# Strided attention rows loaded in pieces of 64 and 8, 48 and 6, and three times 18 rows

## The chip, the cores and the metric

The kernel runs on one core of a Trainium2 chip. The metric is the device time of one execution in microseconds (us), lower is better. Times come from repeated timed runs; one further execution was recorded by the hardware profiler, and all views of the profile below are of that execution.

## The reference

Inputs are `q`, `k`, `v` of shape (8 batches, 8 heads, 576 positions, 64), and two weight matrices. Attention is sparse: heads 0 to 3 look back over at most 32 positions (local), heads 4 to 7 at every position of the same remainder modulo 32 (strided). A feed-forward layer with a squared ReLU follows.

```
mask_local   = (rel >= 0) & (rel < 32)                    # rel = query position - key position
mask_strided = (rel >= 0) & (key % 32 == query % 32)
attn = softmax(where(mask, q @ k.T / 8, -1e9)) ; a = attn @ v
x = a.transpose(0, 2, 1, 3).reshape(4608, 512)
h = x @ w_in                                              # 512 -> 2048
out = (relu(h) ** 2) @ w_out                              # 2048 -> 512, float32
```

## The kernel before

**Two kinds of work on TensorE.** The feed-forward layer is cut in nine chunks of 512 rows of `x`. For each chunk `mm1` makes 16 groups of four matmuls (128x512) with `w_in` (L707), ScalarE applies the ReLU (L713), VectorE squares it into `g_sb` (L714), and `mm2` makes 16 groups of four matmuls with `w_out` (L729). A chunk is thus 32 groups, and all of them form one list of 288 groups, numbered from 0. Between the groups a hand-written list, `PLAN`, places the steps of attention: a line such as `44: S9! D8.0 k20v` means that these steps are issued just ahead of group 44. Batch 0, whose attention must be ready before the first chunk can start, is written out in `BATCH0`. TensorE works strictly in that order, and so does every other engine on its own part of it.

**Loads.** All loads that change float32 to bfloat16 on the way are issued by GpSimd (POOL in the profile), in the order in which the steps come. Each load is given one of eight completion semaphores in turn, so a load is issued only when the load eight places ahead of it has landed; POOL stands still until then, and whatever stands behind on POOL waits with it. DMA transposes and the stores of the output are issued by SyncE (SP), also in order.

**The strided heads.** A row of 32 consecutive positions of one head is 32 x 64 = 2048 numbers. A batch has 18 such rows in each head, so 72 rows in the four strided heads. The steps that the change touches:

- `r1q`, `r1k` (`load_str_rows`, L312) and `C2q` to `C7k` (`load_str_tall`, L349) load the 72 rows of `q` or `k` into `q_t` or `k_t` (72 partitions x 2048). For batch 1 they are transposed on TensorE (`step_TS`, L321); from batch 2 on SP transposes the tile by DMA (`transpose_str`, L354, steps `X`) into `qT_s` and `kT_s`. From `kT_s` VectorE spreads the keys into `kb` (`step_K`, L365 and L368), which the scores read (`step_SS`, L574). `q_t` and `k_t` have one buffer each: the next load waits until the transpose of the last has ended.
- `U1` to `U7` (`load_v_str`) load `v` for the strided heads into `v_st` (54 partitions): the 54 rows of heads 4 to 6 (L390), and head 7 as three overlapping stretches of its 18 rows, 768 numbers each, in one transfer with a source of 3 x 18 rows (L393). VectorE spreads the tile into `vb` (`spread_v_str`, L397).
- `load_v0` loads `v` of batch 0's strided heads into `vs0`, a part of `g_sb` (L608: 72 partitions x 4 x 512), ahead of the loads of `w_in` (L425).

Other loads that the prediction names: `w_out` in four parts (L429; part i is first needed by the groups of chunk 0's `mm2` with that part), local `v` into `vl` (L418, 24 x 64 numbers on 128 partitions), local `q` and `k` into `q_l` and `k_l` (L278), which SP transposes into `qT` and `kTl` (L378).

Of the kernel before, what the change touches and what calls it, by code (L numbers as in the profile page):

```python
# [156 lines left out]
def kernel(  # L157
# [9 lines left out]
    nc = tc.nc  # L167
    B, H, S, D = q.shape
    d_model, d_ff = moe_w_in.shape
    T = B * S  # L170
    STRIDE = 32
    NA = S // STRIDE
# [3 lines left out]
    NJ = 8  # L176
    RH = STRIDE // NJ
    SP_ = RH * NA
# [4 lines left out]
    NG = 5  # L183
    NB = NP2 + NG + 1
    W3 = 3 * NA
    RW = STRIDE * D
# [65 lines left out]
    vs0 = b0[0:SP_, 0:n_s].rearrange("p (u n d) -> p u n d", u=2, d=D)  # L252
# [47 lines left out]
    NP3 = 4 * SP_ // QL  # L300
    str_rows = {}

    def load_str_rows(b, name):
        src = q if name == "q" else k
        if b == 0:
            c = 4 if name == "q" else 8
            t = w_out_b[0:QL, c:c + NP3, :]
            nc.gpsimd.dma_start(out=t, in_=src[b, 4:8].rearrange("h (p j) d -> (h p) (j d)", j=NJ)
                                .rearrange("(s p) c -> p s c", p=QL))
        else:  # L310
            t = str_rows_t[name][0:SP_]
            nc.gpsimd.dma_start(out=t, in_=src[b, 4:8].rearrange("h (m r) d -> (h m) (r d)", r=STRIDE))  # L312
        str_rows[b, name] = t

    def step_TS(b, name, g, copy):
# [30 lines left out]
    def load_str_tall(b, name):  # L346
        src = q if name == "q" else k
        t = str_rows_t[name]
        nc.gpsimd.dma_start(out=t[0:SP_], in_=src[b, 4:8].rearrange("h (m r) d -> (h m) (r d)", r=STRIDE))  # L349
        big[b, name] = t  # L350

    def transpose_str(b, name):
# [34 lines left out]

    def load_v_str(b):
        t = v_st.tile([W3, 2 * NB * D], BF16, name="v_st")
        nc.gpsimd.dma_start(out=t[:, 0:RW], in_=v[b, 4:7].rearrange("h (m r) d -> (h m) (r d)", r=STRIDE))  # L390
        src = v[b, 7]
        src = bass.AP(src.tensor, src.offset, [[2 * NG * D, 3], [RW, NA], [1, 2 * (NG + 1) * D]])
        nc.gpsimd.dma_start(out=t[:, RW:2 * NB * D], in_=src)  # L393
        v_str[b] = t

    def spread_v_str(b, par, copy):
# [3 lines left out]
    def load_v_local_sw(b):  # L400
        i = (2 * b) % NV
        t = vl_all[:, i:i + 2]
        nc.gpsimd.dma_start(out=t[32:128, :, :, :, 0:D].rearrange("p u h t d -> p (u h t) d"),
                            in_=v[b, 0:4].rearrange("h (t p) d -> p (h t) d", p=QL))
        for u in range(2):
            st.setdefault(4 * b + u, {})["v"] = t[:, u]
# [198 lines left out]

    def load_v0():
        load_v_local_sw(0)
        nc.gpsimd.dma_start(  # L608
            out=vs0.rearrange("p u n d -> p (u n d)").rearrange("p (h c) -> p h c", h=4),
            in_=v[0, 4:8].rearrange("h (p j) d -> p h (j d)", j=NJ))  # L610

    def step_N(u):
        e, hw = st[u]["e"], S // 2
# [158 lines left out]
    def run_step(word):  # L772
# [36 lines left out]
        elif op == "P":  # L809
            first_part(*([int(x) for x in y] for y in arg.split(".")))  # L810
        elif op == "H":
            shift_v_local(int(arg[:-1]), ENG[arg[-1]])
        elif op == "C":
            load_str_tall(int(arg[:-1]), arg[-1])
        elif op == "Q":
            load_qk_rows(int(arg[:-1]), arg[-1])
        elif op == "X":
            transpose_str(int(arg[:-1]), arg[-1])
        elif op == "Y":
            transpose_local(int(arg))  # L820
        elif op == "V":
            load_v_local_all(int(arg))
        elif op == "U":
            load_v_str(int(arg))
        elif op == "B":
            spread_v_str(int(arg[0]), int(arg[1]), ENG[arg[2]])
        elif op == "l":
            load_qk_local_sw(int(arg[0]), [int(x) for x in arg[2:].split("+")], arg[1])
        elif op == "r":
            load_str_rows(int(arg[0]), arg[1])  # L830
        elif op == "i":
            load_w_in(int(arg))
        elif op == "o":
            load_w_out(int(arg))
        elif op == "z":
            late_constants()
        else:
            raise ValueError(word)
# [25 lines left out]
    nc.scalar.preload_act_table_set("natural_log_exp_and_others")  # L864
    load_qk_hw(0)
    load_str_rows(0, "q")
    make_identity(nc, ident)
    load_str_rows(0, "k")
    nc.vector.memset(idle, 0.0)
    nc.vector.memset(mask_loc, 1.0)  # L870
# [21 lines left out]
    for i in range(2):  # L892
# [8 lines left out]
                            NEG, -NEG, op0=ALU.mult, op1=ALU.add)  # L901
    load_qk_local_sw(0, (1,))
    load_v0()
    for i in range(4):
        load_w_in(i)
# [34 lines left out]
    for line in PLAN.strip().splitlines():  # L940
        n, words = line.split(":")
# [40 lines left out]
```

## Time and profile before

| what | us |
|---|---|
| median of 3 timed runs | 300.25 (299.5 to 300.93) |
| the profiled execution, its own time | 298.88 |
| its span, first to last instruction | 297.2 |
| TensorE busy with matmuls (PE) | 289.2 (97%) |
| VectorE (DVE) busy | 177.9 (60%) |
| ScalarE (ACT) busy | 172.3 (58%) |
| GpSimd (POOL) busy, issuing loads included | 72.4 (24%) |

The granted clock of TensorE was 1.000 throughout. The median of the timed runs is 1.37 us above the profiled execution, and the profiled execution's own time is 1.68 us above its span. PE is TensorE's matmuls and PEld its weight loads; a name such as `PE psb L729` is the engine, the tile that is written and the line. "Idle before" is the time in which an engine stood still ahead of an instruction, and the name behind the arrow is what ended that.

### The profile page before, as it was taken

The numbers are of one execution on the slowest core, as the hardware profiler recorded it, in microseconds if no ns is written. First come the engines' busy times: TensorE is split into PE (matmuls) and PEld (weight loads), VectorE is DVE, ScalarE is ACT, GpSimd is POOL, SyncE is SP. The second block draws the span as 40 slices with busy tenths as digits, with TensorE's granted clock in tenths as the row PEclk, the third lists the DMA queues.
The fourth block names the chain that finished last, engine by engine and source line by source line (L and its number), as shares of the span: only waits on it lengthen the run. The fifth ranks groups of instructions, "written<-read, shape, count | busy, mean of one in ns | idle before, by whom it ended". The sixth has DMA issues, their size and how long they took to land.

```text
span 297.2 us, 5652 instructions
## 1 busy us (share of the span) xinstructions
PE 289.2 (97%) x2136; PEld 146.0 (49%) x2172; DVE 177.9 (60%) x460; ACT 172.3 (58%) x325; POOL 72.4 (24%) x105
## 2 busy tenths in 40 slices
PE   7999999999999999999999999999999999999996
PEld 2644555555544444544455445544554444444444
DVE  6866779677779694697267936785475534104400
ACT  3858846686667735783477447745665257217511
POOL 8846643006404027083303710000000000000000
PEclk9999999999999999999999999999999999999999
DMA  8999999999999999999999999521011100010012
GB/s 157 181 209 204 194 198 187 158 225 140 129 166 176 157 211 164 159 136 157 186 145 150 174 186 142 89 57 71 35 23 55 73 35 0 35 74 35 0 71 73
DMA packets 93131, 37.28 MB, mean 125 GB/s; under 512 B 78956, under 2 KB 87238, under 8 KB 93104
## 3 DMA queue, kind: packets, MB, share of 16 engines
q0 software_dynamic: 54448, 18.82, 58.1%
q1 hardware_dynamic: 38512, 18.03, 32.6%
q8 instruction: 17, 0.28, 0.4%
q14 instruction: 10, 0.08, 0.1%
q10 hardware_dynamic: 144, 0.07, 0.1%
HBM read 38.21 MB, written 9.44 MB: 160 GB/s over the span
## 4 chain that ended last, share of the span: by engine, by line
PE 92%; DVE 3%; ACT 2%; issue 2%; DVEq 0%; ACTq 0%
PE psb L729 39%; PE psb L707 39%; PE psb L667 2%; PE psb L453 1%; PE psb L764 1%; PE psb L588 1%; PE psb L505 1%; PE psb L754 1%; PE psb L585 1%; PE psb L574 1%; ACT r L713 1%; PE psb L550 1%; DVE g_sb L714 1%; PE psb L475 1%; PE psb L331 0%
## 5 line engine op out<-in xcount | busy, mean ns | idle before, releaser
L707 PE MATMUL psb<-xt,w_in_b 128*128 128x512 bf16 x558 | 132.1, 379 | 1.4 <-ACT xt L692 0.4
L729 PE MATMUL psb<-w_out_b,g_sb 128*128 128x512 bf16 x542 | 125.3, 379 | 1.3 <-issue 0.6
L713 ACT ACTIVATE r<-psb 128x512 bf16<-128x512 f32 x144 | 85.5, 600 | 37.5 <-PE psb L707 34.0
L714 DVE TENSOR_TENSOR g_sb<-r 128x512 bf16<-128x512 bf16 x144 | 60.7, 423 | 72.8 <-ACT r L713 71.7
L707 PEld LDWEIGHTS <-w_in_b 128*128 128x128 bf16 x576 | 53.4, 98 | 59.0 <-issue 1.6
L729 PEld LDWEIGHTS <-g_sb 128*128 128x128 bf16 x560 | 51.8, 98 | 57.2 <-DVE g_sb L714 0.3
L733 ACT COPY y<-psb 128x512 f32<-128x512 f32 x35 | 20.6, 589 | 53.2 <-PE psb L729 50.2
L598 DVE TENSOR_TENSOR xt<-psb,rv 64x144 bf16<-64x144 f32 x84 | 34.1, 406 | 8.0 <-ACT rv L591 6.8
L590 ACT ACTIVATE rv<-psb 128x432 f32<-128x432 f32 (+1 forms) x21 | 10.5, 501 | 9.8 <-PE psb L585 9.8
L673 DVE TENSOR_TENSOR x_l<-psb,rinv 96x384 bf16<-96x384 f32 x28 | 15.5, 554 | 1.0
L349 POOL DMA_DIRECT2D q_t<-in_q_dram x6 | 3.4, 567 | 43.4 <-DMA qT_s<-q_t 26.0
L604 DVE TENSOR_TENSOR xt<-psb,rv 64x270 bf16<-64x270 f32 (+1 forms) x28 | 10.9, 432 | 3.8 <-ACT rv L591 3.6
L575 ACT ACTIVATE e<-psb 128x432 bf16<-128x432 f32 (+1 forms) x21 | 10.4, 496 | 3.7 <-PE psb L574 3.7
L418 POOL DMA_DIRECT2D vl<-in_v_dram x7 | 10.3, 1475 | 8.6 <-DMA vl<-in_v_dram 6.2
L278 POOL DMA_DIRECT2D k_l<-in_k_dram x16 | 11.7, 736 | 2.8 <-PE psb L453 2.4
L278 POOL DMA_DIRECT2D q_l<-in_q_dram x16 | 11.6, 732 | 1.0 <-DMA k_l<-in_k_dram 1.0
L561 ACT ACTIVATE e<-psb 128x384 bf16<-128x384 f32 x24 | 9.6, 511 | 3.4 <-PE psb L550 3.4
L591 ACT ACTIVATE rv<-rv 128x432 f32<-128x432 f32 (+1 forms) x21 | 11.2, 533 | 0.7
L557 DVE TENSOR_TENSOR e<-e,mask_all 128x576 bf16<-128x576 bf16 x16 | 6.7, 459 | 7.2 <-ACT e L561 7.1
L667 PEld LDWEIGHTS <-e 128*128 128x128 bf16 x168 | 8.6, 101 | 4.6
L349 POOL DMA_DIRECT2D k_t<-in_k_dram x6 | 3.2, 535 | 28.0 <-DMA kT_s<-k_t 25.7
L667 PE MATMUL psb<-vl,e 128*128 128x65 bf16 x168 | 9.5, 195 | 0.1
(117 smaller groups left out, 215.9 us busy)
## 6 DMA issues: line engine op xcount, KB each, us to landing
out_dram<-y SPq DMA_DIRECT2D x35, 256.0 KB, 2.8
vl<-in_v_dram POOLq DMA_DIRECT2D x7, 384.0 KB, 12.4
w_out_b<-in_moe_w_out_dram POOLq DMA_DIRECT2D x4, 512.0 KB, 15.1
q_t<-in_q_dram POOLq DMA_DIRECT2D x7, 288.0 KB, 5.8
k_t<-in_k_dram POOLq DMA_DIRECT2D x7, 288.0 KB, 6.1
v_st<-in_v_dram POOLq DMA_DIRECT2D x7, 216.0 KB, 7.9
w_in_b<-in_moe_w_in_dram POOLq DMA_DIRECT2D x2, 704.0 KB, 13.1
k_l<-in_k_dram POOLq DMA_DIRECT2D x16, 72.0 KB, 8.1
```

The costliest lines, as they stand in the source:

```text
L278: nc.gpsimd.dma_start(out=t[:, :, hh, :], in_=src[b, 2 * p + hh].rearrange("(t p) d -> p t d", p=QL))
L590: nc.scalar.activation(rv, pn, AF.Ln)
L591: nc.scalar.activation(rv, rv, AF.Exp, scale=-1.0)
L598: nc.vector.tensor_tensor(to[:, :, NJ * part:NJ * (part + 1), par], of, by, op=ALU.mult)
L604: nc.vector.tensor_tensor(t, of[:, g:, :, lo:lo + k], by[:, g:, :, lo:lo + k], op=ALU.mult)
L667: nc.tensor.matmul(po[0:m, n, :], e[:, c:c + m], rhs[:, NL * part + n, 0:D + 1], start=True, stop=True)
L673: nc.vector.tensor_tensor(x, po[0:QL, :, 0:D], rinv[0:QL].to_broadcast([QL, NL, D]), op=ALU.mult)
L707: nc.tensor.matmul(ph, w_in_b[:, kk, 128 * ff:128 * (ff + 1)], xt[kk][:, 512 * c:512 * (c + 1)], start=(kk == order[0]), stop=(kk == order ...
L713: nc.scalar.activation(r, ph, AF.Relu)
L714: later(1, lambda: nc.vector.tensor_tensor(g[:, ff, :], r, r, op=ALU.mult))
L729: nc.tensor.matmul(py, g[:, ff, 128 * j:128 * (j + 1)], w_out_b[:, ff, :], start=(ff == 0), stop=(ff == 15))
L733: nc.scalar.copy(y, py)
```

## The change

Every load of strided rows is split in pieces. A new helper, `load_even`, splits a transfer after the largest multiple of 16 partitions: 72 rows become 64 and 8, 54 rows become 48 and 6. The load of head 7's values becomes three transfers of 18 rows. The bytes that are moved, the tiles and the order of the steps stay as they are.

```diff
+    def load_even(out, src):
+
+        n = out.shape[0] // 16 * 16
+        for r in (slice(0, n), slice(n, out.shape[0])):
+            nc.gpsimd.dma_start(out=out[r], in_=src[r])
+
     def load_str_rows(b, name):
...
             t = str_rows_t[name][0:SP_]
-            nc.gpsimd.dma_start(out=t, in_=src[b, 4:8].rearrange("h (m r) d -> (h m) (r d)", r=STRIDE))
+            load_even(t, src[b, 4:8].rearrange("h (m r) d -> (h m) (r d)", r=STRIDE))
...
     def load_str_tall(b, name):
         src = q if name == "q" else k
         t = str_rows_t[name]
-        nc.gpsimd.dma_start(out=t[0:SP_], in_=src[b, 4:8].rearrange("h (m r) d -> (h m) (r d)", r=STRIDE))
+        load_even(t[0:SP_], src[b, 4:8].rearrange("h (m r) d -> (h m) (r d)", r=STRIDE))
...
     def load_v_str(b):
         t = v_st.tile([W3, 2 * NB * D], BF16, name="v_st")
-        nc.gpsimd.dma_start(out=t[:, 0:RW], in_=v[b, 4:7].rearrange("h (m r) d -> (h m) (r d)", r=STRIDE))
-        src = v[b, 7]
-        src = bass.AP(src.tensor, src.offset, [[2 * NG * D, 3], [RW, NA], [1, 2 * (NG + 1) * D]])
-        nc.gpsimd.dma_start(out=t[:, RW:2 * NB * D], in_=src)
+        load_even(t[:, 0:RW], v[b, 4:7].rearrange("h (m r) d -> (h m) (r d)", r=STRIDE))
+        src = v[b, 7].rearrange("(m r) d -> m (r d)", r=STRIDE)
+        for g in range(3):
+            c = 2 * NG * D * g
+            nc.gpsimd.dma_start(out=t[NA * g:NA * (g + 1), RW:2 * NB * D], in_=src[:, c:c + 2 * (NG + 1) * D])
...
     def load_v0():
         load_v_local_sw(0)
-        nc.gpsimd.dma_start(
-            out=vs0.rearrange("p u n d -> p (u n d)").rearrange("p (h c) -> p h c", h=4),
-            in_=v[0, 4:8].rearrange("h (p j) d -> p h (j d)", j=NJ))
+        load_even(vs0.rearrange("p u n d -> p (u n d)").rearrange("p (h c) -> p h c", h=4),
+                  v[0, 4:8].rearrange("h (p j) d -> p h (j d)", j=NJ))
```

The lists of instructions of TensorE, VectorE, ScalarE and SyncE are the same before and after, apart from the semaphores that they wait for: who waited for one load now waits for its pieces. GpSimd issues 36 loads more, 123 in place of 87: seven each for `q`, `k` and the first 54 rows of `v`, fourteen for head 7's values, one for `vs0`. With eight semaphores in turn, eight loads are under way at most, as before, but a piece takes a place as a whole load does. After the change all pieces that `load_even` issues have line 307, and the three transfers of 18 rows line 400; lines further down are higher by 6 or 7.

## The prediction

> **What bounds the kernel now.** The page first: who is busy, and when.
>
> ```profile
> span 297.2 us, 5652 instructions
> ...
> PE   7999999999999999999999999999999999999996
> ...
> POOL 8846643006404027083303710000000000000000
> ...
> DMA  8999999999999999999999999521011100010012
> ```
>
> TensorE is full in every slice but the first and the last. The DMA engines are full too, but only up to 180 us, and POOL issues its last load at 171 us. So the question is whether PE ever waits for a load. The waits of PE, then the only wait of its weight loads that a DMA ended:
>
> ```profile
> PE psb L764 <- DVE xt L869: 1.3, 1, 1.3
> PE psb L729 <- issue: 0.6, 4, 0.2
> PE psb L505 <- DVE kTl L460: 0.4, 1, 0.4
> PE psb L648 <- ACT e L509: 0.4, 1, 0.4
> PE psb L707 <- ACT xt L692: 0.4, 1, 0.4
> ```
>
> ```profile
> PEld L331 <- DMA w_out_b<-in_k_dram: 0.3, 1, 0.3
> ```
>
> These end before 17 us, except the 0.6 of issue. PE waits for a load once, 0.3 us at 8.7 us, for rows of batch 0 that the change doesn't touch and that are issued ahead of all that it does. The other early waits are chains of ScalarE and VectorE (a copy into `xt`, an exponential). The starts of consecutive 128x512 matmuls lie 216 ns apart from 20 us to 290 us, with loads running or not, so PE gains nothing from calmer DMA engines either. Faster loads have next to nothing to win in this execution; the change matters only if a load that comes just in time now comes late.
>
> How the loads land: each counts its semaphore up sixteen times, once for each DMA engine, and the trace has the time of every count. For the 72 rows of `q_t` issued at 67.59 us the counts come at 69.45, 70.70, then fourteen from 71.36 to 73.10: one engine has no rows, one has few, fourteen have most. For `vs0` (issued 6.87) four come from 11.54 to 12.12 and twelve from 12.79 to 13.91. By the Trainium skill, "DMA: Bandwidth & Descriptors", section "Why a DMA increments its semaphore by 16 and not by 1", a load uses the largest number of engines up to 16 that divides its rows, and some direct copies from GpSimd all 16 with the rows rounded up (five each of 72); the counts agree with twelve engines for `vs0` and with the rounding for `q_t`. The unevenness adds up while the queue is full: the first and the last count of a load lie 2.3 us apart at `w_in` (landed 15.47) and 10.8 at the `k_t` that lands at 51.63.
>
> **The change part by part.** POOL first: 36 loads more to issue. The nearest rows:
>
> ```profile
> L393 POOL DMA_DIRECT2D v_st<-in_v_dram x7 | 4.4, 633 | 1.4 <-DMA xt<-in_k_dram 0.7 <-DMA xt<-in_q_dram 0.6
> L390 POOL DMA_DIRECT2D v_st<-in_v_dram x7 | 3.7, 533 | 4.8 <-DVE vb L397 1.5 <-DVE rinv L672 1.5 <-DMA w_in_b<-in_moe_w_in_dram 1.2
> L349 POOL DMA_DIRECT2D q_t<-in_q_dram x6 | 3.4, 567 | 43.4 <-DMA qT_s<-q_t 26.0 <-DMA qT<-q_l 15.9 <-DMA vl<-in_v_dram 1.4
> ```
>
> 54 rows cost 533 ns and 72 rows 567, so the rows hardly count, and a piece of 6, 8 or 18 rows is taken at 0.5 us (bounds 0.2, if the rows counted in full the way these two differ and something fixed were shared, and 0.63, the dearest row). 36 x 0.5 = 18 us on POOL: 72.4 becomes about 90 of 297. That lies beside PE; its cost is loads issued later.
>
> Start, to 17 us. `vs0` in two pieces puts the four loads of `w_in` 0.5 us later, the first from 7.61 to 8.1. It lands at 15.47, 7.9 us after its issue, because the engines work at what was issued before; it is queue-bound, and the 0.5 is hidden by that backlog. With sixteen engines even on 64 of the 72 rows I take its landing at 15.2 to 15.6. Its first matmul starts at 16.26, released by the `xt` copy of ScalarE, so both bounds cost nothing: 0.0.
>
> 17 to 52 us. Up to `w_out` part 2 six pieces more are in line (`vs0`, `q_t`, `k_t`, one of `v_st`'s 54 rows, two of head 7's), and the waits for eight places push POOL: stepping through POOL's order with the landings of before, `vl` goes from 21.4 to about 24 us, `w_out` part 2 from 28.7 to about 34.6 and part 3 from 31.7 to about 37.5. At 34.6 the engines still hold work until about 39 (`v_st` landed at 39.00 and 40.39), so they don't run dry. What counts is the sum of each engine's rows. If the small pieces go round all engines, the laggards vanish: `w_out` part 2 has its middle counts at 41.1 and its last at 42.92, and I gain up to 1.4 us there. If the small pieces always fall on the same low engines, these carry five rows of 72 as before, and part 2 moves by -0.2 to +0.5 us. The needs, by PE's timeline:
>
> ```profile
> 42.00 1.02 PE L729 MATMUL psb<-w_out_b,g_sb 128*128 128x512 bf16 x4
> 43.27 1.89 PE L729 MATMUL psb<-w_out_b,g_sb 128*128 128x512 bf16 x8
> 45.60 1.67 PE L729 MATMUL psb<-w_out_b,g_sb 128*128 128x512 bf16 x7
> 47.67 3.61 PE L729 MATMUL psb<-w_out_b,g_sb 128*128 128x512 bf16 x16
> ```
>
> Part 2 starts at 43.27 (spare 0.35 us), part 3 at 47.67 against a landing at 46.99 (spare 0.68). Cost 0.0, at worst 0.5 - 0.35 = 0.15.
>
> 52 to 180 us. `qT_s` lands at 67.04 and PE wants it at 67.58 (spare 0.54); `kT_s` lands at 88.55, and VectorE needs it to fill `kb` for 91.79 (spare 1.1 by its timeline); `kTl` lands at 140.20 for 140.69 (0.49), `vl` at 150.41 for 151.45 (1.04). All other landings are 2 us or more ahead. The first rests on `k_t` and `q_t` landing at 51.6 and 50.0, which come 0.2 late to 1.2 early by the paragraph above. For the others POOL is later by 0.5 us for each extra piece ahead, two to seven in a stretch, while the engines have a backlog or wait for a transpose. At 142 us the eight places bind:
>
> ```profile
> POOL vl L418 <- DMA vl<-in_v_dram: 6.2, 1, 6.2
> ```
>
> The second `vl` waits there for the first, which landed at 141.73. With `k_t` and `q_t` as two loads each, the last load of `q_l` has to wait for that landing, 0.72 of issue, and `vl` comes behind it: issued 0.7 to 1.25 later than 142.27, against the spare of 1.04. Cost 0 to 0.2.
>
> Sum on the profiled execution: 0 + 0 + 0.1 + 0.1 = 0.2, so 298.88 becomes 299.1. The median of the timed runs lies 1.37 above it, which gives 300.4.
>
> **Rivals.** *The eight places run out (slower).* A piece of 8 rows holds a place like a megabyte does, so POOL stalls behind one slow load more often. It decides if `vl` at 142.27 goes over 1.04 us later. The price hangs on how long `vl` sticks beside DMA transposes: issue to landing was 12.4 us there (129.34 to 141.73), 18.8 in the worst case (49.36 to 68.16), 6.4 in the best. In between, 3 us later less the spare is a stall of 2 to 2.5: 302.7; the full 6.4 gives 306. For it: the lines of POOL's waits. Against: POOL is behind by 0.5 to 1 us there, not by 3.
>
> *A piece costs what a whole load does (slower).* Loads of 72 KB issued one behind the other land 0.46 to 0.58 us apart (`k_l` and `q_l`, 114 to 119 us):
>
> ```profile
> k_l<-in_k_dram POOLq DMA_DIRECT2D x16, 72.0 KB, 8.1
> ...
> v_st<-in_v_dram POOLq DMA_DIRECT2D x7, 81.0 KB, 8.2
> ```
>
> Six pieces at 0.5 put `w_out` part 2 3.0 us later, less up to 1.4 from the laggards, less 0.35: a stall of 1.3 to 2.7, 302.2. Against: those loads are made of 576 short runs each, a piece of 18 at most. The Trainium skill ("DMA: Bandwidth & Descriptors", "Anatomy of one DMA") gives every load from GpSimd a fixed 2.0 us, and under "Rules for kernel authors" advises against splitting one transfer by partitions; six times 2.0 would be 12 us. The 0.46 to 0.58 us between whole loads shows that loads in a line don't pay it in turn.
>
> *Laggards vanish and timed runs gain (faster).* The trace's PE waits hold 0.3 us of loads, all out of reach. Only if the 1.37 us between timed and profiled runs were PE waiting for late loads could evenness win them: 298.7. Nothing in the profile shows it.
>
> *The change doesn't even the load* (small pieces on fixed engines). Then landings stay within 0.5 us, and the time is that of the forecast.
>
> **How the numbers follow.** About 0.5% (1.5 us) is what a measurement can tell from no change. Forecast, with the fixed-engine case in it: 0.66, own range 299.5 to 301.7. Eight places: 0.17 at 302.7. Pieces as whole loads: 0.10 at 302.2. Faster: 0.07 at 298.7. The chances are 0.07 faster, 0.66 same, 0.27 slower. The range leaves out the faster case and the long tail of the stalls: 299.3 to 303.0.
>
> **What would show it.** Right: PE's waits as before, 216 ns between matmuls, `w_in` landed by 15.6, `w_out` part 2 by 43.3; first and last counts of the `k_t` load near 51 us closer than 10.8 us; POOL busy near 90. Wrong: PE or PEld waiting for a DMA past 17 us, above all L729 near 43, the local scores near 140 and L667 near 151; a `vl` issued after 143.5; or a median under 298.7, which would mean that PE waited in timed runs for loads that the profile shows in time.

## The result, and the profile after

The changed kernel takes 303.24 us in the median (300.66 to 305.56, 15 runs), the kernel before 299.73 (299.34 to 301.9, 15 runs). Run against run the ratio is 1.0092, 95% interval 1.0066 to 1.0119: slower by 0.9%. The prediction's range was 299.3 to 303.0, so 303.24 lies just above it, far from the 300.4 that it held likeliest. Ratios here leave out runs more than 1.5% above the fastest of their own kernel. The profiled execution took 304.57 us, with a span of 302.4.

The page of the changed kernel, the lines that answer to those of before:

```profile
span 302.4 us, 5706 instructions
...
PE 292.7 (97%) x2136; PEld 147.8 (49%) x2172; DVE 181.5 (60%) x460; ACT 172.7 (57%) x325; POOL 90.2 (30%) x141
...
PE   7899999999999999999999999999999999999996
...
POOL 8664693403917119073331950000000000000000
PEclk9959999999999999999999999999999999999999
DMA  7999999999999999999998998812110110010012
```

Three things differ: POOL is busy for 90.2 us instead of 72.4, which is the 18 us that the extra loads were to cost it; the clock row has a 5 in the third slice, where it was 9 before; and the DMA engines, at 5 and 2 tenths in slices 26 and 27 before, are at 8 and 1: the loads end later. PE itself still looks full, and VectorE (DVE), at 181.5 us instead of 177.9, is busy longer with the same instructions.

The waits of PE in the changed kernel (engine, tile, line, what it waited for: us in total, times, the longest):

```profile
PE psb L770 <- DVE xt L875: 1.3, 1, 1.3
PE psb L654 <- DMA vl<-in_v_dram: 1.1, 1, 1.1
...
PE psb L581 <- DVE kb L371: 0.6, 1, 0.6
```

And PE in four stretches of that execution (columns: stretch, its length, busy time and instructions, granted clock, DMA share, GB/s):

```profile
12.00:16.00 4.00, 2.62 (x42) 1.00 1.30 195
16.00:20.00 4.00, 3.40 (x47) 0.57 1.18 209
20.00:24.00 4.00, 4.00 (x29) 0.58 1.20 207
24.00:28.00 4.00, 4.00 (x19) 1.00 1.25 209
```

This execution lost its time early: the local `vl` of batch 0 landed at 14.15 instead of 12.11, PE stood still for it, and from 16 to 24 us its clock was granted little more than half. The first matmul with `w_out` starts at 37.65 instead of 33.39, so 4.3 of the 5.2 us are gone by then. It would be easy to stop here. But `vl` is issued ahead of every load that the change touches, and the experiments show the same start in a kernel whose loads are whole up to 45 us. Most of what the profile of this one execution shows need thus not be what the 15 runs have in common.

The loads show what comes back in other kernels with such pieces. The stretch from 36 to 48 us, all engines (the last three columns: granted clock, DMA share, GB/s), before:

```profile
36.00:48.00 12.00, 11.89 (x131) 6.84 (x128) 9.81 (x28) 6.08 (x13) 4.79 (x7) 1.00 1.25 203
```

and after:

```profile
36.00:48.00 12.00, 11.33 (x141) 6.45 (x141) 10.26 (x22) 6.93 (x16) 9.98 (x13) 1.00 1.16 175
```

The engines moved 28 GB/s less over 12 us, 336 KB, which is 1.7 us at 203 GB/s. The `k_t` of batch 2, whose loads stand at the end of that stretch, landed at 53.57 instead of 51.63. The reason is in POOL's order (start, length, line, load; in brackets how long POOL stood still ahead of it, and for what):

```profile
29.12 0.55 POOL L307 DMA_DIRECT2D v_st<-in_v_dram  x1 [0.68 <-DMA xt<-in_k_dram]
30.19 0.56 POOL L307 DMA_DIRECT2D v_st<-in_v_dram  x1 [0.52 <-DMA q_t<-in_q_dram]
30.74 0.51 POOL L400 DMA_DIRECT2D v_st<-in_v_dram  x1
33.22 0.50 POOL L400 DMA_DIRECT2D v_st<-in_v_dram  x1 [1.96 <-DMA w_out_b<-in_moe_w_out_dram]
34.04 0.68 POOL L400 DMA_DIRECT2D v_st<-in_v_dram  x1 [0.32 <-DMA k_t<-in_k_dram]
...
36.57 0.79 POOL L436 DMA_DIRECT2D w_out_b<-in_moe_w_out_dram  x1 [0.27 <-PE psb L512]
```

Five pieces of together 297 KB (192, 24 and three times 27) take five of the eight places, each wait for a DMA is for the load eight places ahead, and `w_out` part 2, 512 KB by the same count, is issued at 36.57 instead of 28.71. POOL's memsets of `vb` and `kb`, which stand among these loads, are late with them: the one of `kb` starts at 40.44 instead of 32.41.

### The profile page after: what moved, and what is told of

It reads as the page before. It is cut to its first block, busy times and chain, and to the rows that moved or that the text cites. A ratio compares the mean times of both kernels' runs of the same rounds, so it can differ in the third digit from the quotient of the medians.

```text
span 302.4 us, 5706 instructions
## 1 busy us (share of the span) xinstructions
PE 292.7 (97%) x2136; PEld 147.8 (49%) x2172; DVE 181.5 (60%) x460; ACT 172.7 (57%) x325; POOL 90.2 (30%) x141
## 4 chain that ended last, share of the span: by engine, by line
PE 86%; DVE 5%; DMA 3%; ACT 2%; issue 2%; POOL 1%; DVEq 0%; ACTq 0%; POOLq 0%
PE psb L713 38%; PE psb L735 38%; DMA vl<-in_v_dram 3%; PE psb L673 1%; PE psb L595 1%; ACT r L719 1%; PE psb L760 1%; PE psb L581 1%; DVE g_sb L720 1%; PE psb L592 1%; DVE kb L371 1%; PE psb L557 1%; PE psb L460 1%; PE psb L695 1%; DVE e L534 1%
## 5 line engine op out<-in xcount | busy, mean ns | idle before, releaser
L713 PE MATMUL psb<-xt,w_in_b 128*128 128x512 bf16 x558 | 133.5, 382 | 0.9
L739 ACT COPY y<-psb 128x512 f32<-128x512 f32 x35 | 20.6, 590 | 53.2 <-PE psb L735 50.2
L307 POOL DMA_DIRECT2D q_t<-in_q_dram x14 | 7.8, 566 | 31.2 <-DMA qT_s<-q_t 30.5
L307 POOL DMA_DIRECT2D k_t<-in_k_dram x14 | 7.8, 561 | 25.4 <-DMA kT_s<-k_t 21.2
L611 DVE TENSOR_TENSOR xt<-psb,rv 64x270 bf16<-64x270 f32 (+1 forms) x28 | 10.9, 432 | 3.8 <-ACT rv L598 3.6
L400 POOL DMA_DIRECT2D v_st<-in_v_dram x21 | 10.7, 517 | 3.6 <-DMA w_out_b<-in_moe_w_out_dram 2.0
```

Source lines behind the costliest of these rows:

```text
L307: nc.gpsimd.dma_start(out=out[r], in_=src[r])
L611: nc.vector.tensor_tensor(t, of[:, g:, :, lo:lo + k], by[:, g:, :, lo:lo + k], op=ALU.mult)
L713: nc.tensor.matmul(ph, w_in_b[:, kk, 128 * ff:128 * (ff + 1)], xt[kk][:, 512 * c:512 * (c + 1)], start=(kk == order[0]), stop=(kk == order ...
L739: nc.scalar.copy(y, py)
```

## The experiments

Each kernel was timed beside the kernel before on the same chip. "Span" below is the median over the runs with a mean granted clock of 0.997 or more, less that of the kernel before in the same call (298.2, 297.9 and 298.05 us); "low clock" counts the other runs; "outside" is the time of an execution less its span.

| kernel | extra loads | ratio, 95% interval | span | low clock | outside |
|---|---|---|---|---|---|
| before | 0 | | | 5 of 86 | 1.71 |
| changed | 36 | 1.0092 (1.0066 to 1.0119) | +2.5 | 6 of 15 | 2.16 |
| e1, `vs0` whole | 35 | 1.0123 (1.0076 to 1.0169) | +2.35 (2 runs) | 4 of 6 | 2.00 |
| e2, `vs0` alone | 1 | 1.0028 (1.0010 to 1.0047) | +0.9 | 1 of 12 | 1.71 |
| e3, `v_st` alone | 21 | 1.0013 (0.9981 to 1.0045) | +0.05 | 2 of 12 | 1.72 |
| e4, `q_t`, `k_t` alone | 14 | 1.0030 (1.0002 to 1.0058) | +1.0 | 3 of 12 | 1.73 |
| f1, empty loads | 36 | 1.0074 (1.0038 to 1.0110) | +1.85 | 2 of 12 | 2.16 |
| f2, late pieces | 28 | 1.0033 (1.0002 to 1.0063) | +0.6 | 1 of 12 | 2.04 |
| f3, early pieces | 8 | 1.0019 (0.9984 to 1.0055) | +1.05 | 5 of 11 | 1.71 |
| f4, bytes first | 36 | 1.0072 (1.0040 to 1.0104) | +1.85 | 2 of 12 | 2.16 |
| h1, late empty loads | 36 | 1.0013 (0.9986 to 1.0040) | +0.15 | 1 of 12 | 1.77 |
| h4, early empty loads | 8 | 1.0057 (1.0030 to 1.0085) | +1.65 | 3 of 12 | 1.70 |

(For the changed kernel the spans of before are not known run by run; 298.0 is taken, its median less 1.7. One run each of before and of f3, at 781 and 1075 us, is left out of the columns on span and clock.)

**Which part of the change.** Four kernels undo or do one part. Of their theories, A puts the loss at the start with `vs0`, B at the eight places, and C takes it for chance between executions.

```diff
# e1: the changed kernel, load_v0 as before
-        load_even(vs0..., v[0, 4:8]...)
+        nc.gpsimd.dma_start(out=vs0..., in_=v[0, 4:8]...)
# e2: the kernel before, load_even in load_v0 only
# e3: the kernel before, the pieces of load_v_str only
# e4: the kernel before, load_even in load_str_rows and load_str_tall only
```

> The changed kernel with the load of vs0 (batch 0's strided values) whole again; all other loads stay in pieces. Theory A (the start: the split of vs0 makes batch 0's local values vl land late, PE waits about 1.2 us for them near 13 us and the granted clock drops afterwards): the time of before, 299.5 to 300.2, vl landed by 12.3 and PE without a wait for a DMA near 13 us. Theory B (the pieces of q_t, k_t and v_st use up the eight places and delay loads after 17 us): still 302 to 304. Theory C (the start is late by chance in any kernel, the change only takes away spare time): in between, 300.5 to 302.5, with a wide scatter of the runs.

> The kernel before with only the load of vs0 in pieces of 64 and 8. Theory A: about all of the loss, 302 to 304, vl landed after 13 us, in part of the runs with a clock below 1.0. Theory B: 299.5 to 300.2. Theory C: 300 to 302.

> The kernel before with only the loads of v_st in pieces (48, 6 and three times 18 rows). Theory A: 299.5 to 300.2, no new PE wait. Theory B: 1 to 2.5 us over before, with a PE wait after 40 us. Theory C: 299.5 to 301.

> The kernel before with only the loads of q_t and k_t in pieces of 64 and 8. Theory A: 299.5 to 300.2, no new PE wait. Theory B: 0.5 to 2 us over before, with a PE wait after 40 us. Theory C: 299.5 to 301.

The pieces of `vs0` are not needed for the loss: without them the kernel is as slow (1.0123), so A falls. But alone they cost 0.28%, where B expected nothing, and the pieces of `v_st` add 0.05 us, where B expected 1 to 2.5; C expected less than e1's 303.24 us. No theory holds by itself. One extra load costs 0.28%, 21 cost 0.13% and 14 cost 0.30%: the loss is not a price per piece. The three add up to 0.7%, inside the interval of the change, so nothing shows that the parts cost more together than one by one. In e1's profile PE waits for what the prediction gave a spare of 0.54 us:

```profile
PE psb L581 <- DMA qT_s<-q_t: 2.7, 1, 2.7
```

`qT_s` landed at 72.28 there, and at 68.73 to 68.83 in e2, e3 and e4, against 67.04 before. In e4 `kTl` was late too: PE stood still for 1.2 us until 113.12.

**Places, or the shape of the pieces.** In f1 all loads are whole. Behind each stands as many nearly empty loads as the change adds, so POOL's order and the use of the eight places are those of the changed kernel, but no load has another shape.

```diff
+    def take_place():
+        i = 8 * taken[0]
+        taken[0] += 1
+        nc.gpsimd.dma_start(out=spare_places[:, i:i + 8], in_=moe_w_in[0:16, 0:8])
...
         nc.gpsimd.dma_start(out=t[0:SP_], in_=src[b, 4:8]...)
+        take_place()
```

> All loads whole as before; behind each load that the change splits stands an extra load of 16 rows x 8 elements (0.5 KB each) into memory that nobody reads, as many as the change has extra pieces (36), in the same positions of POOL's order. Theory P (places: what costs time is that extra loads hold places, so POOL stands still, fewer bytes are under way between 35 and 45 us and the strided rows of batch 2 land late): the k_t that lands at 51.63 us before lands at 53 to 54.5, w_out part 2 is issued at 35.5 to 37 instead of 28.71, qT_s lands after 69, PE waits 1 to 4 us between 64 and 95 us, ratio 1.006 to 1.013. Theory S (the shape of the pieces costs: rows on other engines, small pieces that take as long as whole ones): nothing of shape is changed here, so k_t lands at 51.6 to 52.2 and the ratio is 1.000 to 1.003.

Theory S falls. The empty loads alone cost 0.74%, and POOL and the loads go as in the changed kernel: `w_out` part 2 issued at 36.78, the engines at 178 GB/s from 36 to 48 us, `k_t` landed at 53.93, `qT_s` at 69.30. The stretch of f1, and PE at the matmuls that read `qT_s`:

```profile
36.00:48.00 12.00, 11.72 (x121) 6.42 (x122) 10.50 (x26) 5.65 (x12) 10.26 (x14) 1.00 1.14 178
```

```profile
69.34 0.36 PE L587 MATMUL psb<-qT_s,kb 128*128 128x54 bf16 x8 [0.46 <-DMA qT_s<-q_t]
```

PE's wait was expected at 1 to 4 us between 64 and 95 us; the profiled execution, the fastest of the twelve, shows 0.46 there. Its longest past 10 us is another: 0.87 us until 17.12, ahead of the first matmul with `w_in`, which had landed at 17.07.

**When.** f2 keeps the pieces that are issued after 45 us, f3 those before it.

```diff
# f2: load_v0 and load_str_rows as before, and
+        if b > 2: load_even(...)                  # load_str_tall; else whole
+        if b > 1: load_even(...) and 3 x 18 rows  # load_v_str; else whole
# f3: load_even in load_v0 and load_str_rows, and
+        if b <= 2: load_even(...)                 # load_str_tall; else whole
+        if b == 1: load_even(...) and 3 x 18 rows # load_v_str; else whole
```

> Of the change only what is issued after 45 us: the loads of vs0, of the rows of batch 1, of v_st of batch 1 and of q_t and k_t of batch 2 are whole, all later ones in pieces (28 of the 36 extra loads stay). Theory P with its place at 25 to 45 us: k_t lands at 51.6 to 52.2, ratio 1.000 to 1.004, what is left coming from vl and kT_s near 90 and kTl near 112. Theory N (every extra load costs a little wherever it stands: 2.8 to 3.6 us over 36 is 0.08 to 0.10 each): ratio 1.007 to 1.010.

> The other half: only the loads of vs0, of the rows of batch 1, of v_st of batch 1 and of q_t and k_t of batch 2 are in pieces (8 extra loads), all later ones whole. Theory P with its place at 25 to 45 us: POOL as in the changed kernel up to 45 us, k_t landed at 53 to 54.5, qT_s after 69, ratio 1.005 to 1.012. Theory N: 8 x 0.1 us, ratio 1.002 to 1.003.

28 pieces late cost 0.6 us of span, 8 pieces early 1.05, so it is not the number (theory N wanted 2 us or more from f2). But f3 missed what theory P expected of the time and the landings: its interval holds no change, and in its profiled execution `k_t` landed at 52.33 and `qT_s` at 67.73, ahead of PE: span 297.9. Its runs go from 299.58 to 305.5 us, and by the ratio f2 loses no less than f3, so this pair does not settle when the loss arises. In f2's profile `k_t` landed at 53.09, later than expected, though its loads are whole up to there. That execution has the start of the changed kernel's: `vl` landed at 14.23, and

```profile
12.00:16.00 4.00, 2.62 (x42) 1.00 1.20 204
16.00:20.00 4.00, 3.40 (x48) 0.54 1.17 208
```

**The same with empty loads.** h4 has the 8 early ones of f1, h1 all 36 behind the last real load.

```diff
# h4: take_place() behind the loads of vs0, of the rows of batch 1 and, once for b == 2, in
#     load_str_tall; three in load_v_str for b == 1
# h1: 197: s7.0 f      (f: 36 x take_place())
```

> The kernel before with all its loads whole, and an empty load behind each of those of vs0, the rows of batch 1 and q_t and k_t of batch 2, three behind v_st of batch 1: the 8 early ones of f1_empty_places alone. Theory P: w_out part 2 issued after 35 us, k_t of batch 2 landed between 52.2 and 54, full-clock spans 1.0 to 1.9 us longer than before, ratio 1.003 to 1.007, and 1.72 us outside of the span. Theory N: 8/36 of 1.7 us, ratio 1.001 to 1.002.

> The kernel before with all its loads whole and where they were; the 36 empty loads (16 rows x 8 elements, 0.5 KB each, read by nobody) are issued in one line behind the last real load, after 180 us. Theory P (extra loads cost because they hold places between 15 and 60 us): the span is as before, within 0.3 us, and PE waits nowhere longer. Theory N (each costs wherever it is): 1.7 us or more in the span. Apart from both: in the kernels run so far the time of an execution exceeds its span by 1.71 to 1.73 us with 21 extra loads or fewer and by 2.00 to 2.16 with 28 to 36; if the number of loads in the program sets that, it is 2.16 here, ratio 1.0015 in all; if it was POOL's early delay, 1.72, ratio 1.000.

This is the clearest pair. The same load of half a kilobyte costs nothing that can be told from no change when it is issued after 175 us (36 of them: +0.15 us of span, ratio 1.0013) and 0.57% when 8 of them stand between 7 and 44 us. At full clock h4's nine spans go from 298.7 to 300.4 us, h1's eleven from 297.8 to 298.8 but for one. In h4 `w_out` part 2 was issued at 36.39 and `k_t` landed at 53.06.

Up to that issue POOL had waited 8.2 us for landings in h4's profile and 1.8 before, and spent 3.1 us on issuing six empty loads; for VectorE it waited less. So most of the delay is waiting for places, but POOL's own time for issuing is part of it, and no run has the one without the other.

h1 shows something else. Up to 175 us it has the order of before; yet in its profiled execution `vl` of batch 0 landed at 13.41, `k_t` of batch 2 at 53.17 and `qT_s` at 69.15, PE waited 0.29 and 0.34 us for `qT_s` and `kb` until 69.19 and 93.90, and the span was 299.7, the longest of its eleven runs at full clock. The landings thus move by 1 to 2 us from one execution to the next without any change. What separates the kernels is seen only over several profiles:

| profiled execution | `vl` of batch 0 landed | `w_out` part 2 issued | GB/s, 36 to 48 us | `k_t` landed | `qT_s` landed |
|---|---|---|---|---|---|
| before | 12.11 | 28.71 | 203 | 51.63 | 67.04 |
| h2 (below), order of before | 12.43 | 29.18 | 202 | 51.18 | 67.48 |
| h3 (below), order of before | 12.34 | 28.93 | 204 | 51.80 | 67.59 |
| h1, order of before | 13.41 | 29.53 | 203 | 53.17 | 69.15 |
| f2, whole up to 45 us | 14.23 | 31.53 | 203 | 53.09 | 69.28 |
| e2 | 12.73 | 30.26 | 202 | 52.58 | 68.73 |
| e3 | 12.71 | 34.22 | 198 | 52.27 | 68.73 |
| e4 | 12.55 | 32.91 | 206 | 51.27 | 68.83 |
| f3 | 12.25 | 35.60 | 188 | 52.33 | 67.73 |
| h4 | 12.89 | 36.39 | 180 | 53.06 | 68.52 |
| f1 | 12.41 | 36.78 | 178 | 53.93 | 69.30 |
| e1 | 12.66 | 37.07 | 181 | 53.84 | 72.28 |
| changed | 14.15 | 36.57 | 175 | 53.57 | 70.79 |
| f4 (below) | 13.39 | 28.66 | 197 | 52.14 | 69.84 |

Two things go with a late `k_t`: a late `vl` at the start (h1, f2: 1.5 us), with no change ahead of it, and the early extra loads. Among the executions whose `vl` landed by 12.9, `k_t` landed at 51.5 in the mean of three with the order of before and at 53.3 in the mean of four with seven or eight early extra loads (f3, h4, f1, e1): 1.8 us, about the 1.7 worked out above from the bytes. A late `qT_s` doesn't need a late `k_t`: in e4 `k_t` landed at 51.27 and `qT_s` at 68.83, because both transposes took over 12 us from issue to landing, 9.6 and 10.9 before.

**Bytes first.** f4 is the changed kernel with two entries of the plan exchanged, so that a large load takes the place that a piece had.

```diff
-5: o1 U1 mbg
-6: o2 l2k8+9 mv0g o3 mk0g
+5: o1 o2 U1 mbg
+6: l2k8+9 mv0g o3 mk0g
```

> The changed kernel, with the load of w_out part 2 (1 MB) issued ahead of the five pieces of v_st of batch 1 instead of behind them, so that the places hold more bytes while POOL waits. Theory P: w_out part 2 is issued near 29 us and lands by 42, the engines keep over 190 GB/s from 35 to 42 us, k_t of batch 2 lands at 51.6 to 52.8, qT_s before 69, ratio 1.002 to 1.007; a v_st that lands near 44 instead of 41 may cost up to 0.7 us at the first product with vb near 49 us. Theories S and N: the pieces are the same, so k_t stays at 53 to 54.5 and the ratio at 1.009 to 1.012.

The landing came back as forecast: `w_out` part 2 issued at 28.66, `k_t` landed at 52.14, and

```profile
36.00:48.00 12.00, 10.68 (x116) 5.65 (x115) 11.08 (x25) 5.05 (x11) 9.03 (x11) 1.00 1.21 197
```

The time came back only in part: 1.0072, whose interval overlaps that of the change. `qT_s` was expected before 69 and landed at 69.84: here too the two transposes took over 12 us. More loads beside them don't explain it, since e4 has the same loads under way beside its slow transposes as f3 beside its fast ones (9.6 and 10.8 us). And PE never waited for `qT_s` in this execution: neither `k_t` nor `qT_s` cost it time.

**Where PE loses the time.** How much later than in the profile of before PE starts three groups of matmuls (us; for before, the times themselves):

| profiled execution | first with `w_out` | third group with `vb` | scores of batch 2, with `qT_s` |
|---|---|---|---|
| before | 33.39 | 47.51 | 67.58 |
| h2 | +0.47 | +0.47 | +0.47 |
| h3 | +0.22 | +0.39 | +0.39 |
| h1 | +1.16 | +1.16 | +1.60 |
| f2 | +4.21 | +4.21 | +4.21 |
| e2 | +0.85 | +0.85 | +1.19 |
| e3 | +0.47 | +0.87 | +1.19 |
| e4 | +0.60 | +0.92 | +1.29 |
| f3 | +0.43 | +0.73 | +0.72 |
| h4 | +0.86 | +1.50 | +1.50 |
| f1 | +0.64 | +1.14 | +1.76 |
| f4 | +1.14 | +2.72 | +2.71 |
| e1 | +0.58 | +1.27 | +4.74 |
| changed | +4.26 | +5.18 | +5.18 |

Two of the three steps don't tell the kernels apart. The start differs without any change (h1, f2), and up to `qT_s` h1 and e2 lose 0.3 to 0.4 us and e1 3.5, while f3, h4, f4 and the changed kernel lose nothing. The step between, from 33 to 48 us, does: 0.3 to 1.6 us in all eight with extra loads at `q_t`, `k_t` or `v_st` by then, at most 0.17 in the other five. What happens in it is on VectorE. Before, POOL's memset of `kb` is long over when VectorE copies `kT_s` into the other `kb`:

```profile
32.41 1.29 POOL L862 MEMSET kb<- 128x1408 f32 x1
35.73 0.38 DVE L365 COPY kb<-kT_s 64x864 bf16<-64x864 bf16 x1
```

In h4 a memset and in the changed kernel an issue and a memset fall beside that copy, and PE waits behind it:

```profile
37.88 1.27 POOL L879 MEMSET vb<- 128x1408 f32 x1
38.16 1.24 DVE L376 COPY kb<-kT_s 64x864 bf16<-64x864 bf16 x1
39.54 0.36 PE L590 MATMUL psb<-qT_s,kb 128*128 128x54 bf16 x8 [0.47 <-DVE kb L379]
```

```profile
39.99 1.98 DVE L371 COPY kb<-kT_s 64x864 bf16<-64x864 bf16 x1
40.44 1.29 POOL L868 MEMSET kb<- 128x1408 f32 x1
43.02 0.36 PE L581 MATMUL psb<-qT_s,kb 128*128 128x54 bf16 x8 [0.56 <-DVE kb L371]
```

In f4 such a copy took 2.08 us instead of 0.24 beside POOL's memset at 39.66, and PE stood still for 1.11 us until 41.92 for what VectorE did next. Exchanging the loads brought the bytes back, but not POOL's memsets to their old place. So the extra loads cost PE time by a second way that no theory here had named: they move POOL's other work beside VectorE's copies. No run moves the memsets alone, so what share of the timed loss this makes isn't shown.

**What a wait of PE costs.** Two kernels put one wait of known size at 246 us, where no load runs.

```diff
+    def pause(n):
+        pw = bank("pt")
+        nc.tensor.matmul(pw, ident, w_in_b[:, 0, 0:512], start=True, stop=True)
+        for _ in range(n):
+            nc.vector.tensor_copy(pause_t, pw)
+        nc.tensor.matmul(bank("pt")[:, 0:128], pause_t[:, 0:128], ident, start=True, stop=True)
...
+230: p2        # h2_pause_short; p5 in h3_pause_long
```

> The kernel before with one wait put into PE's order near 240 us, where no load runs: a matmul into a spare bank, two VectorE copies of that bank (about 0.66 us each), a matmul that reads the copy; neither result is used. PE stands still for 1.4 to 1.9 us. Theory C (a wait of PE of over 1 us is itself followed by some us of half clock, as at 13 us of the changed kernel's profile): the loss is 3 to 5 us and the granted clock of the run is below 0.997 in most runs. Rival (the half clock of those profiles has another cause than the wait): loss 1.6 to 2.2 us, clock 1.0 as before.

> The same with five copies: PE stands still for 3.4 to 4.0 us. Theory C: loss 5 to 8 us, clock below 0.997 in most runs. Rival: 3.6 to 4.3 us, clock 1.0.

PE stood still longer than was expected, 2.38 and 4.56 us. Its timeline in h2 and then in h3, and two windows of h3:

```profile
248.46 0.23 PE L775 MATMUL psb<-ident,pause_t 128*128 128x128 bf16 x1 [2.38 <-DVE pause_t L774]
248.53 8.80 PE L708 MATMUL psb<-xt,w_in_b 128*128 128x512 bf16 x40
```

```profile
249.28 0.29 PE L775 MATMUL psb<-ident,pause_t 128*128 128x128 bf16 x1 [4.56 <-DVE pause_t L774]
249.36 11.54 PE L708 MATMUL psb<-xt,w_in_b 128*128 128x512 bf16 x40
```

```profile
249.00:252.00 3.00, 2.72 (x8) 0.50 0.00 0
252.00:256.00 4.00, 4.00 (x14) 0.64 0.00 0
```

Behind 2.38 us of standing still the 40 matmuls take 8.80 us, 220 ns each: full clock. Behind 4.56 us they take 11.54, and the first thirteen run at half clock. In the timed runs all six of h3 have a clock below 0.997 (ratio 1.0227, 1.0199 to 1.0254: 6.8 us for 4.9 of wait and added matmuls), of h2 two of six (1.0111, 1.0076 to 1.0146; 2.85 us of span at full clock). So the theory of the clock (C of these two) holds for the long wait; for the short one it holds at most in some executions. By the Trainium skill, "TensorE: Matmul & The Clock Gate", section "Part 1: The HAM clock gate (the "warmup" mystery)", TensorE falls to half clock after an idle window of about 3.4 us that runs freely. The 4.56 us agree. In e1's profile the clock fell behind PE's wait of 2.66 us for `qT_s` (0.60 from 73 to 77 us). The drops at 16 us of the changed kernel and of f2 came where no single wait of PE after 10 us passed 1.1 us and PE was busy for 2.62 us of 4, so there PE was not idle for a whole stretch of that length; what set them off isn't shown.

## Why the prediction was right or wrong

*The likeliest case failed.* It gave 300.4 us, with 0.2 us for the change; the change costs 3.5. That the time still lies at the edge of the range is in part luck: the rival "the eight places run out" had 302.7, but tied to the `vl` at 142 us, where PE lost nothing. The median of three runs to which the forecast was added, 300.25, was also 0.5 above the median of 15.

*The step that failed* is in the paragraph on 17 to 52 us: "At 34.6 the engines still hold work until about 39 (`v_st` landed at 39.00 and 40.39), so they don't run dry." In part they did: 175 GB/s from 36 to 48 us instead of 203. It counted when work would end, not how many bytes were under way while POOL stood still. From it came the second error, "`k_t` and `q_t` landing at 51.6 and 50.0, which come 0.2 late to 1.2 early": they came 1.9 and 2.3 late in the profiled execution, and `k_t` 1.8 by the table's means. Against a spare of 0.54 at `qT_s` that can be a wait: 0.46 us in f1, 2.66 in e1. It was none in the profiles of the changed kernel, f3, f4 and h4, because PE was late itself or `qT_s` in time.

*A second step failed* with it: of POOL's 18 us the prediction said "That lies beside PE; its cost is loads issued later." POOL's work also lay beside VectorE's copies into `kb` and `vb`, which took up to 2.08 us instead of 0.24 to 0.52, and PE waited behind them: 0.56 us in the changed kernel, 0.47 in h4, and 1.11 in f4 for VectorE's next result. The prediction had no term for it.

*The rival that came nearest* was tied to the `vl` at 142 us, and "POOL is behind by 0.5 to 1 us there" spoke against it. POOL does wait longer for a place there, 8.2 us instead of 6.2, and the second `vl` is issued at 149.6, which is 144.4 without the 5.2 us by which the whole execution is late; but PE waits for none of it. Places did run out, between 14 and 34 us.

*POOL's own delay* was right in kind and a size too small: `w_out` parts 2 and 3 were forecast at 34.6 and 37.5 us and came at 36.57 and 39.70 (35.60 and 39.18 in f3). POOL's busy time, 90, was right.

*A spare was taken from one execution.* `qT_s` 0.54, `kTl` 0.49, and for `vl` of batch 0, which landed at 12.11 with VectorE beginning on it at 12.22, none was worked out at all. Over the profiles with the order of before this `vl` lands at 12.1 to 13.4 (14.2 in f2), and the `k_t` of batch 2 at 51.2 to 53.2. In h2, with that order, PE waits 1.1 us for the very `kTl` that had 0.49 to spare. A spare smaller than such scatter is used up in some executions before anything is changed.

*The laggards vanish* as forecast: the counts of the `k_t` near 51 us, 10.8 us apart from first to last before (40.80 to 51.63), lie within 2.1 us (51.45 to 53.57). It brought nothing, because before, thirteen of the sixteen counts had come by 50.32, and now the first comes at 51.45. All engines are late alike, and the last count follows them.

*A piece costs what a whole load does* was rightly given a small chance: the five pieces of `v_st` land 0.22 to 0.35 us apart (39.82 to 40.90), the two of `q_t` 0.4. The Trainium skill's advice against splitting one transfer by partitions, which the prediction cited from "DMA: Bandwidth & Descriptors", "Rules for kernel authors", agrees with the change being slower by 0.9%. The fixed price per load that the prediction named beside it is not what the pieces pay here: they land closer together than that.

*The start* was put at nothing. `w_in` landed at 16.77 instead of "15.2 to 15.6", in an execution with a late `vl`; f2 has that `vl` and e1 keeps the loss with `vs0` whole. The spare was thin all the same: in f3 `w_in` landed at 16.97 and PE waited 0.86 us for it, where in h1, h2 and h3 it landed at 15.41 to 16.35.

*Nobody forecast 0.44 us* that lies outside the span: 2.16 instead of 1.71 us in the mean over the runs of the changed kernel. It is there with 28 to 36 extra loads spread over the kernel, not with 21 or fewer, and not with 36 in a line at the end (1.77). Neither the number of loads nor POOL's early delay (h4: 1.70) sets it alone; its cause stays open.

In sum, the 3.5 us between the medians are about 2.5 us of span at full clock, 0.44 outside of the span, and the rest from more executions with a stretch of half clock. Such executions are 22 of 68 in the six kernels with seven or eight early extra loads and 7 of 110 in before, f2 and h1, so they too go with the change; the runs without a trace don't show why. Of the 2.5, empty loads in the same places make 1.85, 8 early ones 1.65; that the remaining 0.65 is the shape of the pieces isn't shown, as the intervals overlap. That extra loads early in POOL's order cost time is shown by h4 against h1 and by f1, with f3 as an exception whose interval is too wide to decide. By which waits they cost it is seen in single executions only: VectorE's stretched copies in all with such loads between 15 and 45 us, a late `qT_s` in some. No kernel here beats the one before, whose PE waits for next to nothing.

## What to carry to other kernels

Where a queue allows a fixed number of loads in flight, count the bytes that these places hold while the issuing engine stands still, not the loads: here a load of half a kilobyte held a place as one of 512 KB does, and cost time where large loads waited behind it. When an engine off the critical path comes late, look at what else it does and beside whom that now falls: instructions of the same form that take longer than before give it away. Compare a shift with the spare of several executions, not of one, since landings here move by 1 to 2 us on their own. And before a cause is read from one profile, look whether the same picture shows up in a kernel that doesn't have the change, and whether PE really waited for the load that came late.

## What the runs showed of the hardware that was not expected

VectorE's copies into `kb` and `vb` were stretched only beside work of GpSimd. In the 14 profiles there are 588 of them. None of the 296 with no memset or load issue of POOL beside it took over 0.38, 0.24 or 0.52 us, depending on its shape; of the other 292, 20 took over 1 us, up to 2.08.

A wait of PE is followed by a price of its own once it is long enough: behind 4.56 us the clock was at half for 5.6 us in the profiled execution, and all six runs of h3 were below full clock, about 2.1 us longer in the span than the wait and the added matmuls; behind 2.38 us no more than two of six were. Loads issued by POOL early in the kernel land 2 us apart from profile to profile with nothing changed ahead of them (`vl` of batch 0: 12.11 to 14.23). And DMA transposes of the same 72 rows took 9.6 to 12.3 us from issue to landing (`kT_s` of batch 2), and 9.6 and 12.1 with the same loads under way beside them (f3 and e4); what sets it stays open.
